# Attention over pooled keys and a gated feed-forward: three ways to raise a gate, two gate functions, and a new written-out order

## The chip, the cores and the metric

The kernel runs on one core of a Trainium2 chip. A core has five engines that each run their own instructions in order and meet through semaphores: TensorE (PE; its weight loads are shown apart as PEld), VectorE (DVE), ScalarE (ACT), GpSimd (POOL) and SyncE (SP), which issues transfers. ScalarE and GpSimd issue transfers on queues of their own as well. Matrix products land in PSUM, which has eight banks. The metric is the device time of one execution in microseconds, the median over runs; lower is better.

## The reference

Shapes: q, k and v are 8 batches x 8 heads x 576 rows x 64, w_in is 512 x 1024, conv_w is 3 x 1024, w_out is 1024 x 512, all float32; the output is 8 x 576 x 512 float32.

```
k_p = k.reshape(B, H, 72, 8, D).mean(axis=3)      # 576 rows -> 72
v_p = v.reshape(B, H, 72, 8, D).mean(axis=3)
scores = (q @ k_p.T) / sqrt(D)
attn = exp(scores - max(scores)); attn = attn / sum(attn)
x = concat_heads(attn @ v_p)                      # 576 x 512 per batch
h = relu(x @ w_in)                                # 576 x 1024
conv_out[s] = sum over k of conv_w[k] * h[s + k - 1]
out = (h * sigmoid(conv_out)) @ w_out
```

## The kernel before

The eight batches form four groups of two. A group's 1152 rows are nine tiles of 128 rows (group 0 is cut into ten, so that its first batch can start alone): 37 tiles of attention in all. For each tile the steps are, with the names and lines of the code before:

- `att_scores` (L530): the scores of all eight heads into two banks of PSUM, on PE.
- `att_max` (L571, instruction L575): the negated maximum of each head's 72 scores, on DVE.
- `att_shift` (L583): adds that maximum. On DVE (L587) it writes the shifted scores to `sd`; on PE (L595) two products with the identity add it in PSUM.
- `att_exp` (L605, instruction L613): one exponential over 128 x 576 on ACT, from `sd` or from PSUM.
- the turn of `e`: five transposes on PE (`att_turn`, L624) and a copy out of PSUM (`att_copy`, L638) by ACT or DVE, or one transposing transfer on SP's queue (`att_send`).
- `att_values` (L649) on PE, `att_divide` (L662, L664) on DVE.
- the turn of `x` in the same two ways: PE (L681) and a copy (L689), or a transfer (`att_out`).

Per batch the feed-forward follows, in eight blocks of 128 of the 1024 columns: `ffn_in` (L694, eight products per block), `ffn_relu` (L703, ACT), the convolution, the gate, and per group the output product `ffn_out` (L910), its copy (L921) and its store (L933, on SP or ACT). Blocks are gated four at a time; (b, f4) names the quarter-of-a-group gate of batch b, half f4.

The convolution of a gate is done in one of two ways. Either PE multiplies with 64 x 64 diagonal matrices (`ffn_conv`, L856), and then half of its results land on the other half of the partitions: ACT writes the tanh of the even blocks into `gT` and of the odd blocks into `tg` (L881), and the raise by one, on DVE, brings the halves of `tg` back to their place (L892, L894). Or it is done by taps: the first on ACT (L829), two on DVE (L831), tanh on ACT (L836), raise on DVE (L842). The second way is taken for (4,1), (5,0), (5,1), (6,0), (6,1) and (7,0). Either way the product with h follows on DVE (L902 or L843). The sigmoid is (1 + tanh(c/2))/2; the relu carries the factor one half. The convolution reads h past its ends from wrapped columns, which POOL copies for batches 4 to 7 (`ffn_wrap`, L778, L779).

The queries arrive as 64-column pieces that PE turns (L483, L487), and DVE or ACT copies them out (`qT`, L501). Keys are pooled with a product on PE (L373, L383) or in three halving sums on DVE (L406), values on DVE (L453), and masked copies of them are made (L457).

Nothing schedules itself: each step is entered into a graph, and the table ORDER names every step and its engine in the order of issue, FORMS the form of a product, PLACES the PSUM bank. An engine waits at its next row until the inputs have come and the buffer is free. Buffers are rings, and their counts stand in one line:

```
rings = {"e": 6, "eT": 3, "negm": 3, "x": 4, "tg": 3, "osb": 5, ...
```

## Time and profile before

| | |
|---|---|
| median of 3 runs | 219.06 us (218.57 to 219.35) |
| the profiled execution | 218.51 us, of which 216.8 us are its span |
| PE / DVE / ACT / POOL busy | 196.2 / 191.3 / 164.3 / 46.8 us |
| PE's granted clock, mean | 0.998 |
| moved by DMA | 32.62 MB, 150 GB/s |

The span is the time from the first to the last instruction of the program, and 1.7 us of the profiled execution lie around it. Busy time counts no register, semaphore or transfer-issuing instruction. A row of a group gives line, engine, operation, output <- input, shapes, count, then busy us and mean ns of one, then the idle time of the engine right before it and what released it. The chain that ended last is followed back from the last instruction, at each step to what released it.

### The profile page before, as it was taken

What the parts mean: (1) busy time and instruction counts of PE and PEld (TensorE: products, weight loads), DVE (VectorE), ACT (ScalarE), POOL (GpSimd) and SP (SyncE); (2) the same over time, 40 slices, a digit from 0 to 9 for tenths busy, and PEclk for the clock granted to TensorE, in tenths of its full rate; (3) what the DMA queues carried; (4) which work ended last, traced back from release to release, by engine and by line L of the source; (5) the groups of instructions that cost most, each with busy time, mean ns of one, the idle gap of its engine ahead of it and who ended that gap; (6) DMA issues with size and microseconds to landing.
All of it is one profiled execution on the core that took longest, in us unless ns stands there. A gap on an engine that the chain in (4) does not pass through costs nothing.

```text
span 216.8 us, 6589 instructions
## 1 busy us (share of the span) xinstructions
PE 196.2 (91%) x2718; PEld 136.2 (63%) x2736; DVE 191.3 (88%) x331; ACT 164.3 (76%) x277; POOL 46.8 (22%) x81
## 2 busy tenths in 40 slices
PE   0487999977999999979999999999999999999991
PEld 0455768866688886756676766676675656644540
DVE  7578987999999999998999999999999999999520
ACT  2057776899889889987578688889999989998220
POOL 7970335041103202000000013113305020530000
PEclk9999999999999999999999999999999999999999
DMA  5999999999999998997565665475576526315665
GB/s 78 156 186 202 208 205 208 207 208 206 206 207 206 205 210 128 178 129 168 115 94 115 137 72 131 83 153 102 115 154 136 134 59 155 81 36 135 150 178 183
DMA packets 48835, 32.62 MB, mean 150 GB/s; under 512 B 28301, under 2 KB 44325, under 8 KB 48805
## 3 DMA queue, kind: packets, MB, share of 16 engines
q0 software_dynamic: 16288, 16.26, 46.2%
q1 hardware_dynamic: 31636, 14.70, 33.5%
q10 hardware_dynamic: 880, 1.25, 2.1%
q8 instruction: 21, 0.34, 0.6%
q14 instruction: 10, 0.07, 0.1%
HBM read 32.52 MB, written 9.44 MB: 194 GB/s over the span
## 4 chain that ended last, share of the span: by engine, by line
PE 75%; DVE 9%; ACT 5%; issue 3%; POOL 3%; DMA 2%; DVEq 0%; POOLq 0%; ACTq 0%
PE psum L910 28%; PE psum L694 26%; PE psum L649 6%; PE psum L856 5%; DVE negm L575 3%; DMA eT<-e 2%; PE psum L624 2%; PE psum L549 2%; ACT qT L501 1%; DVE sd L587 1%; PE psum L681 1%; PE psum L562 1%; ACT eT L638 1%; PE psum L373 1%; PE psum L595 1%
## 5 line engine op out<-in xcount | busy, mean ns | idle before, releaser
L694 PE MATMUL psum<-xT,w_in_sb 128*128 128x288 bf16 x512 | 72.4, 286 | 0.1
L910 PE MATMUL psum<-w_out_sb,gT 128*128 128x512 bf16 (+1 forms) x278 | 66.2, 373 | 0.9 <-issue 0.2
L694 PEld LDWEIGHTS <-w_in_sb 128*128 128x128 bf16 x512 | 47.8, 98 | 15.6 <-issue 0.2
L703 ACT ACTIVATE hT<-psum 128x576 bf16<-128x576 f32 x64 | 40.5, 649 | 8.6 <-PE psum L694 7.0
L910 PEld LDWEIGHTS <-gT 128*128 128x128 bf16 x296 | 27.5, 98 | 26.1 <-issue 0.5
L831 DVE SCALAR_TENSOR_TENSOR tg<-hT,convw,tg 128x576 f32<-128x576 bf16 x48 | 37.2, 817 | 0.4
L575 DVE TENSOR_REDUCE negm<-psum 128x8 f32<-128x576 f32 (+2 forms) x37 | 27.2, 751 | 2.3 <-PE psum L562 1.0
L778 POOL COPY hT<-hT 128x126 bf16<-128x126 bf16 x16 | 9.3, 580 | 92.1 <-ACT hT L703 75.0
L664 DVE TENSOR_TENSOR x<-psum,r 128x512 bf16<-128x512 f32 (+1 forms) x37 | 25.6, 691 | 1.3
L587 DVE TENSOR_TENSOR sd<-psum,negm 128x576 f32<-128x576 f32 x27 | 20.0, 752 | 0.8
L649 PE MATMUL psum<-vm,eT 128*128 128x65 bf16 (+5 forms) x240 | 19.3, 222 | 1.4 <-DMA eT<-e 1.0
L856 PE MATMUL psum<-hT,dw 64*64 64x288 bf16 (+2 forms) x608 | 19.4, 261 | 0.5 <-DVE sd L587 0.3
L613 ACT ACTIVATE e<-sd 128x576 bf16<-128x576 f32 x27 | 18.4, 686 | 0.9 <-DVE sd L587 0.9
L856 PEld LDWEIGHTS <-dw 64*64 64x64 bf16 x608 | 15.4, 107 | 5.2 <-issue 4.3
L829 ACT ACTIVATE tg<-hT,convw 128x576 f32<-128x576 bf16 x24 | 18.4, 775 | 0.1
L649 PEld LDWEIGHTS <-eT 128*128 128x128 bf16 (+1 forms) x240 | 15.1, 100 | 5.3 <-DMA eT<-e 1.2
L921 ACT COPY osb<-psum 128x512 f32<-128x512 f32 x25 | 14.4, 586 | 4.9 <-PE psum L910 3.4
L836 ACT ACTIVATE gT<-tg 128x576 bf16<-128x576 f32 x24 | 16.2, 683 | 1.0 <-DVE tg L831 1.0
L881 ACT ACTIVATE gT<-psum 128x576 bf16<-128x576 f32 x20 | 13.0, 649 | 2.7 <-PE psum L856 2.5
L881 ACT ACTIVATE tg<-psum 128x576 bf16<-128x576 f32 x20 | 13.0, 651 | 2.2 <-PE psum L856 1.5
L902 DVE TENSOR_TENSOR gT<-gT,hT 128x2304 bf16<-128x2304 bf16 x10 | 13.6, 1359 | 0.0
L453 DVE TENSOR_TENSOR v<-v 128x1280 bf16<-128x1280 bf16 (+2 forms) x24 | 13.0, 541 | 0.3
(82 smaller groups left out, 228.6 us busy)
## 6 DMA issues: line engine op xcount, KB each, us to landing
out_dram<-osb SPq DMA_DIRECT2D x54, 128.0 KB, 2.4
v<-in_v_dram POOLq DMA_DIRECT2D x8, 512.0 KB, 19.3
qp<-in_q_dram POOLq DMA_DIRECT2D x7, 576.0 KB, 18.2
kk<-in_k_dram POOLq DMA_DIRECT2D x3, 1152.0 KB, 16.4
w_in_sb<-in_moe_w_in_dram POOLq DMA_DIRECT2D x2, 512.0 KB, 16.0
w_out_sb<-in_moe_w_out_dram POOLq DMA_DIRECT2D x1, 1024.0 KB, 22.0
out_dram<-qp SPq DMA_DIRECT2D x8, 128.0 KB, 2.6
out_dram<-qp ACTq DMA_DIRECT2D x8, 128.0 KB, 2.7
```

The lines of the kernel that those rows point to most:

```text
L575: nc.vector.tensor_reduce(out=a["m"][0:rows], in_=a["s"][0:rows, :, 0:2 * KW].rearrange("p a (h s) -> p a h s", s=Sp), axis=AX.X, op=OP.ma ...
L587: nc.vector.tensor_tensor(out=a["d"][0:rows], in0=a["s"][0:rows, :, 0:2 * KW].rearrange("p a (h s) -> p a h s", s=Sp), in1=a["m"][0:rows]. ...
L613: nc.scalar.activation(out=dst, in_=src, func=ACT.Exp, scale=1.0 / (POOL * 8.0),)
L649: nc.tensor.matmul(out=a["o"][lo:hi, h // 4, (h % 4) * (D + 1):(h % 4 + x1 - x0) * (D + 1)], lhsT=a["eT"][:, j, lo:hi], rhs=buf("vm", b)[: ...
L664: nc.vector.tensor_tensor(out=a["x"][0:rows].rearrange("p (a h d) -> p a h d", a=2, d=D), in0=ov[:, :, :, 0:D], in1=r[0:rows].unsqueeze(3) ...
L694: nc.tensor.matmul(out=banks(ps)[:, j, 0:SC], lhsT=w_in_block(dc, fb), rhs=buf("xT", g)[:, dc, i * S + j * SC:i * S + (j + 1) * SC], start ...
L703: nc.scalar.activation(out=h_of(b)[:, fb].rearrange("p (a s) -> p a s", a=2), in_=banks(ps)[:, :, 0:SC], func=ACT.Relu, scale=0.5,)
L829: nc.scalar.activation(out=acc, in_=h, func=ACT.Identity, scale=w)
L831: nc.vector.scalar_tensor_tensor(out=acc, in0=h, scalar=w, in1=acc, op0=OP.mult, op1=OP.add)
L856: nc.tensor.matmul(out=banks(pss[r ^ c])[c * D:(c + 1) * D, j, lo:hi], lhsT=dw[r * D:(r + 1) * D, tap * n_fb + fb, :], rhs=hT[r * D:(r + 1 ...
L881: nc.scalar.activation(out=t.rearrange("p (a s) -> p a s", a=2), in_=banks(ps)[:, :, 0:SC], func=ACT.Tanh, scale=0.5,)
L910: nc.tensor.matmul(out=bank(ps)[0:rows, columns], lhsT=buf("gT", g)[:, fb, t * P:t * P + rows], rhs=w_out_sb[:, fb, columns], start=(fb == 0),
```

## The change

1. *The raise of a gate* (`raise_gate`, new, L814). It may be done on ACT (L818, an Identity with a bias of one) as well as on DVE (L822). Its parts are no longer bound together: one row may stand apart from the next, with other work between. ACT does six raises in the program as built, five of 64 x 1152 and one of 128 x 1152.
2. *Swap by DMA* (`ffn_swap`, L900): two transfers put the halves of `tg` straight into `gT`, and one raise over all four blocks follows. The table "swap" names (3,0), (5,1), (6,0) and (6,1). The last three are gates by taps ("conv" is 1), and `add_taps` does not read "swap", so the program as built holds two such transfers, both for (3,0), issued on ACT.
3. *Sigmoid* instead of tanh for (5,0) to (7,1): no raise, relu without the half; an odd half of (7,1) is copied to its place (L820). All Sigmoids are ordered behind the last exponential, with one load of a second table of functions.
4. *The shift* ("shift"): by PE for 11 tiles (10 before), by eight exponentials of 72 columns each with the maximum as bias for three tiles, (1,6), (3,3) and (3,5), by DVE for 23 (27 before).
5. *The turns*: of `e` by transfer for 19 tiles (18 before), of `x` for 20 (18 before).
6. *Engines*: five of the 64 relus go from ACT to DVE. Between the two engines' copies out of PSUM, ACT has fewer (eT 15 full and 2 half to 12 and 1, xT 12 and 2 to 8 and 1, qT of 1152 columns 8 to 6, outputs 25 to 23 of `osb`), DVE more. Of the wraps POOL does 20 (32 before), ACT four, and (4,0) and (7,1) have none. ACT issues 24 transfers (11 before), SP ten stores fewer.
7. *Buffers*: e 6 to 4, tg 3 to 4, and the ring "s" goes. The pooling matrix lies in a buffer of `gT`. The factor of the scores moves from the exponential into the pooling matrix. Two products that only filled PE's time go.
8. *The order*: ORDER, FORMS and PLACES are written anew.

What the new order does, at three places. The first is DVE where the gates of batch 0 are raised and first multiplied (L902 before, L916 after); `kk` is the pooling of keys, `x` an attention result divided, `negm` a maximum, `sd` a shift. Before:

```order
L406 TENSOR_TENSOR kk_76<-kk_76 128x9x64
L892 TENSOR_SCALAR gT_119<-gT_119 128x2x576
L894 TENSOR_SCALAR gT_119<-tg_116 64x2x576 x2
L689 COPY xT_112<-psum 128x4x128
L902 TENSOR_TENSOR gT_119<-gT_119,hT_114 128x4x576
L575 TENSOR_REDUCE negm_93<-psum 128x8
```

After:

```order
L822 TENSOR_SCALAR gT_119<-tg_115 64x2x576
L697 RECIPROCAL r_109<-psum 64x8
L699 TENSOR_TENSOR x_104<-psum,r_109 64x512
L697 RECIPROCAL r_108<-psum 128x8
L699 TENSOR_TENSOR x_106<-psum,r_108 128x512
L598 TENSOR_REDUCE negm_96<-psum 128x8
L610 TENSOR_TENSOR sd_127<-psum,negm_96 128x576
L524 COPY qT_80<-psum 128x2x576
L598 TENSOR_REDUCE negm_96<-psum 128x8
L916 TENSOR_TENSOR gT_119<-gT_119,hT_113 128x4x576
```

Between the last raise and the product stand two divisions, two maxima, a shift and a copy of queries. Up to the first product DVE does four shifts and two maxima more than before.

The second is ACT at about the same time: the tanh of batch 0 (L881, L884) and the copies of batch 2's keys (`kT`) and queries (`qT`). Before:

```order
L881 ACTIVATE tg_117<-psum 128x576
L881 ACTIVATE gT_119<-psum 128x576
L689 COPY xT_112<-psum 128x4x64
L501 COPY qT_77<-psum 128x2x576
L501 COPY qT_79<-psum 128x2x576
L501 COPY qT_77<-psum 128x2x576
L501 COPY qT_79<-psum 128x2x576
```

After:

```order
L445 CAST kT_81<-psum 64x4x72 x2
L445 CAST kT_82<-psum 64x4x72 x2
L524 COPY qT_78<-psum 128x2x576
L524 COPY qT_80<-psum 128x2x576
L724 COPY xT_111<-psum 128x4x64
L724 COPY xT_111<-psum 128x4x128
L648 ACTIVATE e_98<-sd_127 128x576
L884 ACTIVATE tg_116<-psum 128x576
L884 ACTIVATE gT_119<-psum 128x576
```

Two copies of queries have left ACT here (DVE has them), and the last tanh of batch 0 stands behind the copies and an exponential.

The third is ACT at the last exponential (L613, L648) and the first gates behind it (L836 a tanh, L851 a Sigmoid). Before:

```order
L613 ACTIVATE e_97<-sd_126 128x2x2x144
L836 ACTIVATE gT_119<-tg_116 128x576
L613 ACTIVATE e_100<-sd_126 128x2x2x144
L921 COPY osb_125<-psum 128x512
L703 ACTIVATE hT_115<-psum 128x576 x2
```

After:

```order
L648 ACTIVATE e_97<-sd_126 128x2x2x144
L851 ACT_TABLE_LOAD
L851 ACTIVATE gT_119<-tg_116 128x576
L851 ACTIVATE gT_119<-tg_118 128x576
L745 ACTIVATE hT_113<-psum 128x576 x2
```

The table is loaded right behind the last exponential, and the gates by taps that stood among the exponentials stand behind it.

The diff, cut to its core:

```diff
-    rings = {"e": 6, "eT": 3, "negm": 3, "x": 4, "tg": 3, "osb": 5,
+    rings = {"e": 4, "eT": 3, "negm": 3, "x": 4, "tg": 4, "osb": 5,
...
+        "conv": {
+            (4, 1): 1, (5, 0): 1, (5, 1): 1, (6, 0): 1, (6, 1): 1, (7, 0): 1,
+        },
+        "swap": {
+            (3, 0): 1, (5, 1): 1, (6, 0): 1, (6, 1): 1,
+        },
...
+        "sigma": {
+            (5, 0): 1, (5, 1): 1, (6, 0): 1, (6, 1): 1, (7, 0): 1, (7, 1): 1,
+        },
...
     ORDER = (
-        6, 10, 2, 4, 28, 16, 14, 20, 24, 22, 34, 8, 26, 42, 36, 44, 12, 32, 30, 40, 92, 56, 18, 98, 38, 95, 58, 101, 104, 64,
+        6, 18, 28, 14, 16, 8, 2, 20, 10, 4, 34, 12, 108, 104, 36, 30, 22, 24, 40, 92, 32, 38, 97, 111, 56, 106, 98, 42, 95, 58,
...
     def att_exp(g, t):
         a, rows = att[g, t], rows_of(g, t)
         e = a["e"] = buf("e", g, t)
+        if graph.chosen("shift", g, t) == 2:
+            for x in range(2):
+                for h in range(4):
+                    at = h // 2 * 2 * KW + x * KW + h % 2 * Sp if a["by_rows"] else (4 * x + h) * Sp
+                    nc.scalar.activation(
+                        out=e[0:rows, at:at + Sp],
+                        in_=a["s"][0:rows, x, h * Sp:(h + 1) * Sp],
+                        func=ACT.Exp,
+                        bias=a["m"][0:rows, x, h:h + 1],
+                        scale=1.0,
+                    )
+            return
...
+    def gate_func(b, fb):
+        return ACT.Sigmoid if graph.chosen("sigma", b, fb // 4) else ACT.Tanh
+
+    def raise_gate(engine, b, fb, out, in_, start=0):
+        sigma = graph.chosen("sigma", b, fb // 4)
+        if engine is nc.scalar:
+            rows = slice(start, start + in_.shape[0])
+            nc.scalar.activation(out=out, in_=in_, func=ACT.Identity, bias=0.0 if sigma else ones[rows], scale=1.0)
+        elif sigma:
+            engine.tensor_copy(out=out, in_=in_)
+        else:
+            engine.tensor_scalar(out=out, in0=in_, scalar1=1.0, scalar2=None, op0=OP.add)
...
+    def ffn_swap(b, f4, queue):
+        g, i = where[b]
+        tg, gate = buf("tg", b, f4), buf("gT", g)[:, 4 * f4:4 * f4 + 4, i * S:(i + 1) * S]
+        gate = gate.rearrange("p (f e) s -> p e f s", e=2)[:, 1]
+        for part in range(2):
+            queue.dma_start(out=gate[part * D:(part + 1) * D], in_=tg[(1 - part) * D:(2 - part) * D])
...
+    for o in sigmas:
+        for e in exps:
+            graph.follow(e, o)
```

More of the change, by code (lines that the diff above doesn't have):

```diff
@@ L967, with add_load @@
[L967 to L980 removed]
+    n_outs = {b: [t for t in range(9) if (t < 4) == (i == 0)] for b, (g, i) in where.items()}
+    kb = H * S * D * 4
+    loads, kp, qp, qTt = {}, {}, {}, {}
+    kk0 = token("kk", 0)
+    kk = {0: kk0}
+    def add_load(kind, b, share=1.0, **part):
@@ L1014 @@
-    p0 = add({"POOL": 1.6}, first("pm"), build_pool_matrix, after=[c1])
-    add_load("q", 0, first("q0"), 4 / 9, cs=slice(0, 4))
-    c0 = add({"POOL": 0.55}, first("ident"), lambda: make_identity(nc, ident))
-    z0 = add({"DVE": 0.3}, soon(), lambda: clear(buffers["kT"][0]))
-    idf = add({"ACT": 0.3}, soon(), lambda: nc.scalar.copy(out=ident_f, in_=ident), after=[c0])
-    cwtok = token("ps")
-    cwp = add({"PE": 0.1}, soon(), lambda: turn_conv_weights(cwtok), after=[idf, cwl], uses=[cwtok], count=2)
@@ new lines, in add_out, with queue @@
+            then(o, lambda o, t=t, sm=sm: ffn_copy(g, t, sm, copier(o)))
+            o = add({"SP": 1.3, "ACT": 1.16}, None, after=[o], uses=[osb], land=(2.4, 0, 1))
+            then(o, lambda o, t=t: ffn_store(g, t, queue(o)))
+    def queue(o):
+        return nc.scalar if o.engine == "ACT" else nc.sync
+    for b in range(B):
+        if b < 2:
+            add_prep_k(b)
+        elif b % 2 == 0:
+            add_pair(b // 2)
+        add_prep_q(b)
+        add_prep_v(b)
+    for b in range(B):
+        for t in n_tiles[b]:
+            add_att(where[b][0], t)
@@ L1343 @@
+    for b in range(B):
+        add_ffn(b)
+        add_out(b)
+    for o in sigmas:
+        for e in exps:
+            graph.follow(e, o)
     with tc.manual_schedule():
```

832 lines of the change are left out of this document (387 added, 445 removed), and 100 rows, old and new, of tables (ORDER, PLACES).

## The prediction

> **What bounds the kernel now.** I read the page's first lines, then busy time by stage, then the chain that ended last, then the groups by shape. The page first:
>
> ```profile
> span 216.8 us, 6589 instructions
> PE 196.2 (91%) x2718; PEld 136.2 (63%) x2736; DVE 191.3 (88%) x331; ACT 164.3 (76%) x277; POOL 46.8 (22%) x81
> PE 75%; DVE 9%; ACT 5%; issue 3%; POOL 3%; DMA 2%; DVEq 0%; POOLq 0%; ACTq 0%
> ```
>
> TensorE carries three quarters of the chain, but VectorE is almost as full, so the share alone decides nothing. The view by stretches, cut where the work changes (PE, PEld, DVE, ACT and POOL busy, each with its count, the granted clock, the DMA share and GB/s):
>
> ```profile
> 0.00:40.00 40.00, 29.06 (x578) 22.61 (x579) 31.12 (x77) 22.47 (x39) 20.55 (x38) 1.00 1.12 179
> 40.00:60.00 20.00, 17.60 (x331) 13.36 (x334) 19.31 (x32) 18.26 (x31) 3.87 (x5) 1.00 1.23 207
> 60.00:92.00 32.00, 31.81 (x562) 25.20 (x560) 30.95 (x57) 29.41 (x50) 4.41 (x6) 1.00 1.13 189
> 92.00:152.00 60.00, 58.35 (x852) 40.78 (x862) 57.79 (x98) 46.64 (x80) 6.63 (x14) 1.00 0.64 118
> 152.00:203.00 51.00, 50.43 (x358) 29.57 (x365) 49.62 (x67) 45.42 (x77) 11.32 (x19) 1.00 0.52 116
> 203.00:217.00 14.00, 8.96 (x49) 4.66 (x48) 2.50 (x4) 2.13 (x4) 0.00 (x0) 0.97 0.58 162
> ```
>
> From 60 to 203 us TensorE idles 0.19 + 1.65 + 0.57 = 2.4 us. A gain must therefore come from less work for it, or from the 10.9 us that it idles before 40, the 2.4 between 40 and 60, and the 1.65 after 92. The chain names what ends those waits (start, duration, engine, tile, line):
>
> ```profile
> 16.40 0.42 PE psum L595 x2
> ...
> 49.48 3.15 ACT qT L501 x3
> ...
> 61.80 0.39 PE psum L624 x5
> 62.18 0.98 PE psum L694 x8
> ...
> 73.61 0.41 PE psum L681 x4
> ...
> 90.59 0.46 DVE gT L894
> ...
> 92.04 4.25 DMA eT<-e
> ...
> 196.72 9.88 PE psum L910 x49
> 206.66 5.37 PE psum L910 x28
> 212.05 0.42 DVE qp L921
> ```
>
> Around 50 ScalarE's copies of the queries stand in the chain, ahead of 92 VectorE's gates, at 92 one turned tile on its way by DMA. The end is TensorE's output product, one copy, and stores.
>
> **The change, part by part.** VectorE first, by shapes (busy us, mean ns, then idle before):
>
> ```profile
> L587 DVE TENSOR_TENSOR sd<-psum,negm 128x576 f32<-128x576 f32 x27 | 20.0, 752 | 0.8
> L894 DVE TENSOR_SCALAR gT<-tg 64x1152 bf16<-64x1152 bf16 x20 | 9.1, 455 | 0.3
> L842 DVE TENSOR_SCALAR gT<-gT 128x2304 bf16<-128x2304 bf16 x6 | 4.7, 790 | 0.4 <-ACT gT L836 0.3
> L892 DVE TENSOR_SCALAR gT<-gT 128x1152 bf16<-128x1152 bf16 x10 | 4.5, 451 | 0.0
> L689 DVE COPY xT<-psum 128x512 bf16<-128x512 bf16 x5 | 2.1, 418 | 0.0
> L501 DVE COPY qT<-psum 128x1152 bf16<-128x1152 bf16 x2 | 1.5, 752 | 0.0
> L921 DVE COPY osb<-psum 128x512 f32<-128x512 f32 x2 | 1.4, 680 | 0.0
> L638 DVE COPY eT<-psum 128x640 bf16<-128x640 bf16 x2 | 1.0, 480 | 0.0
> ```
>
> It loses four shifts (27 to 23), 4 x 0.752 = 3.0. The raises of the gate by one are 9.1 + 4.7 + 4.5 = 18.3 now; afterwards 13 of the half shape, 7 of 1152 and 2 of 2304 columns remain, 5.9 + 3.2 + 1.6 = 10.7, so 7.6 less. It gains five relus out of PSUM, an operation it has no row for: between the 0.680 of a smaller PSUM copy and the 0.817 of a multiply-add, I take the shift's 0.752, the same shape out of PSUM, 3.8 in all. Copies taken from ScalarE: 2.5 of eT 1.2, 2.5 of xT 1.0, two of qT less a short one 1.1, two of outputs 1.4, half an output and a key some 0.9. Sum: -10.6 + 9.4 = -1.2 us.
>
> ScalarE's rows:
>
> ```profile
> L703 ACT ACTIVATE hT<-psum 128x576 bf16<-128x576 f32 x64 | 40.5, 649 | 8.6 <-PE psum L694 7.0 <-DVE x L664 0.8
> L613 ACT ACTIVATE e<-sd 128x576 bf16<-128x576 f32 x27 | 18.4, 686 | 0.9 <-DVE sd L587 0.9
> L921 ACT COPY osb<-psum 128x512 f32<-128x512 f32 x25 | 14.4, 586 | 4.9 <-PE psum L910 3.4 <-remote 1.0 <-PE psum L649 0.3
> L638 ACT COPY eT<-psum 128x640 bf16<-128x640 bf16 x15 | 10.1, 695 | 1.3 <-PE psum L624 1.3
> L501 ACT COPY qT<-psum 128x1152 bf16<-128x1152 bf16 x8 | 8.6, 1125 | 0.8 <-PE psum L483 0.8
> L689 ACT COPY xT<-psum 128x512 bf16<-128x512 bf16 x12 | 7.0, 592 | 0.4 <-PE psum L681 0.2
> L1018 ACT ACT_TABLE_LOAD x1 | 1.3, 1283 | 0.8 <-PEq L1359 0.8
> L398 ACT CAST kT<-psum 64x144 bf16<-64x144 f32 x4 | 1.0, 273 | 6.8 <-DVE kT L294 6.2 <-PE psum L373 0.6
> 204.01 2.50 ACTq L933 DMA_DIRECT2D out_dram<-qp  x4
> ```
>
> It loses five relus (3.2), three whole exponentials net (2.1), 3.5 copies of eT (2.4), 4.5 of xT (2.6), two of qT less one short (1.7) and some 3 other copies (1.9): 13.9. It gains 24 short exponentials, for which the nearest row is the smallest evacuation, 273 ns: 6.6 (lower end 0.2 each, if they overlap as the relus do, 4.8); one table load 1.3; eight short wrap copies by the same 273 ns, 2.2; six raises by the qT row, the nearest of that width, 6 x 1.125 = 6.8; and 13 more transfers issued on its queue at 2.50 / 4 = 0.63 each, 8.1, which are not counted as busy but hold the engine. Sum: +25.0 - 13.9 = +11 us. That leaves ScalarE at 164.3 + 6.9 for the eleven issues of today + 11 = 182 of 217, still not the fullest. The cover is its idle time of 13.4 us between 92 and 152, and 5.6 after it; without that cover each of those operations delays TensorE.
>
> The sixfold raise on ScalarE is dearer in every row: on VectorE the same six are 5 x 0.455 + 0.451 = 2.7. The Trainium skill, "ScalarE: Activation LUTs", section "Rules for kernel authors", says to use VectorE, not ScalarE, for add and multiply. By that rule this part costs 4 us of engine time for nothing; the sum stands at zero for it, because VectorE is the fuller engine here, and by the rule, with ScalarE on the path, it would be up to 4 us worse. No row of before has a raise on ScalarE.
>
> The load of the second table stands between the last exponential and the first Sigmoid. Priced by its row it is 1.3 us once. The same page, section "What ACT_TABLE_LOAD costs", adds a drain of about 1.38 us to the 1283 ns; the row agrees with the 1283, and no row here shows the drain. With it the switch would be an estimated 2.7 us, and ScalarE's sum +12.4.
>
> TensorE, by the chain's rows: one turn of e less (0.39), two of x less (0.82), one shift more (0.42): -0.8. The two fillers that go stand in its idle start and are worth nothing. The turns become transfers, one more of eT and two more of xT, each on SP, whose queue loses ten stores; how a late one hurts the row at 92 shows (4.25 us).
>
> The swap by DMA reaches one gate only: the table names four, but the other three are tap gates, whose code never reads it. For gate (3,0) two transfers on ScalarE's queue replace two half raises and a whole one (1.36) by one raise (0.79) after landing. Their price as latency is bounded by nothing and 4.25, the slowest transfer in the chain; VectorE's taps and maxima and TensorE's input products of the next batch cover it, so zero. POOL gives up 12 wraps and was 78% idle: zero. Fewer buffers for e (6 to 4): an exponential waits for the turn four tiles before it instead of six; the row L613 shows 0.9 us of waits now, all for VectorE's shifts, so zero, with another 0.9 as upper end. The start, from the timeline of POOL:
>
> ```profile
> 5.13 1.33 POOL L319 TENSOR_SCALAR_AFFINE_SELECT mask<-mask 128x15 bf16<-128x15 bf16 x2
> 6.42 1.64 POOL L298 TENSOR_SCALAR_AFFINE_SELECT gT<-gT 64x648 bf16<-64x648 bf16 x2
> ```
>
> POOL now builds the pooling matrix (L298) ahead of the mask. TensorE's first pooling can start 1.3 earlier, VectorE's use of the mask comes 1.6 later; VectorE has as much work before the first maximum as now, so I take zero between -1.3 and +1.6.
>
> Two places remain that the order decides. At 40 to 60 ScalarE has two qT copies less (-2.1 us of the chain's row at 49.48), while VectorE has more ahead of its first gate product: four shifts and two maxima of 0.75 (4.5), copies (0.9) less a few clears (0.4), so 5.0 us. TensorE has, ahead of its first output product, two turns (0.8), an input product (0.98) and more score products, some 2.1 in all. The place is worth between -2.4 (TensorE's idle time gone) and 5.0 - 2.1 = +2.9. The middle is +0.2; I take 0, since VectorE idled between 12 and 40 and can take part of its extra there. At 92 between 0 and -1.65; I take half, -0.8, because other tiles now stand there.
>
> Sum: -0.8 - 0.8 = -1.6. The profiled execution lasted 218.51 (216.8 of span and 1.7 around it), 216.9 by this sum; it lies 0.55 below the median of 219.06, so the median comes to **217.4**. Its own range is 215.4 to 218.4.
>
> **Rivals.** *The order closes the stalls.* The idle 2.4 at 40 to 60 and all 1.65 at 92 go, with TensorE's 0.8: 219.06 - 4.85 = 214.2, and 211.4 if 2.8 of the idle time before 40 goes too. For it: ScalarE's chain at 49.48 is shorter. Against it: VectorE's 19.31 of 20 there.
>
> *VectorE's gates come late in the first stage* (the other side). The 5.0 us more ahead of the first product L902 find no idle time, TensorE arrives 2.1 later and waits 2.9: 219.06 - 0.8 + 2.9 = 221.2. It decides once VectorE absorbs less than 2.1 of the 5.0 in its waits before 40 us. For it: 97% of that stage. Against it: VectorE is lighter afterwards, yet TensorE, dense from 60 on, could not regain what it lost.
>
> *ScalarE becomes the bound.* The Sigmoids wait for the last exponential, ScalarE has 5.6 us free from 152 to 203, and 1.3 of load, one or two raises and four issues (1.3 + 2.2 + 2.5 = 6.0) fill it. If 2.5 reach TensorE: 219.06 - 0.8 + 2.5 = 220.8.
>
> *The parts cancel*: within 0.3% (0.66 us) of 219.06, the bound of what a measurement of this kernel tells from no change.
>
> **How the numbers follow.** 0.44 for the forecast, 0.17 for closed stalls, 0.22 for late gates, 0.11 for ScalarE, 0.06 for cancelling. Faster: 0.44 + 0.17 less 0.02 at the forecast's edge = 0.59; slower: 0.22 + 0.11 less 0.02 that end near zero = 0.31; the same 0.10. The range takes the forecast, most of the stalls' case and both slower ones with their bounds: 211.8 to 221.9.
>
> **What would show it.** TensorE near 195.4 busy, VectorE near 190, ScalarE near 167; the raises on ScalarE near 1.1 us and short exponentials between 0.2 and 0.27; a second table load of 1.28 with ScalarE idle before it or not; two transfers tg to gT and no more; TensorE idle under 2 us between 60 and 203. I am wrong if TensorE idles over 4 us between 40 and 60 waiting for VectorE (late gates), if ScalarE is named as the releaser of TensorE after 150, or if the first maximum comes later than 13 us.

## The result and the profile after

The changed kernel took **225.6 us** (median of 5 runs, 224.97 to 225.68) beside 219.06 us (218.57 to 219.60) for the kernel before: a ratio of 1.0295, 95% interval 1.0262 to 1.0327. It is 6.5 us slower where 1.6 us of gain were forecast, and above the range. The profiled execution lasted 225.55 us, 223.8 of them span. A run's time goes with the mean clock that it is granted: in two sets of runs the changed kernel took 224.9 to 225.7 us in the seven at 0.994 or more (median 225.55), and 227.4 to 228.0 in the four at 0.988 to 0.991.

The page's first lines after:

```profile
span 223.8 us, 6596 instructions
PE 199.2 (89%) x2712; PEld 137.9 (62%) x2729; DVE 190.7 (85%) x327; ACT 164.3 (73%) x290; POOL 36.8 (16%) x70
PE 62%; DVE 14%; ACT 7%; DMA 7%; issue 5%; SPq 2%; POOL 1%; ACTq 0%; DVEq 0%; POOLq 0%
```

VectorE and ScalarE are close to what was forecast. No engine became the bound. What changed is the chain: TensorE's share fell from 75% to 62%; transfers, the issue of transfers on SP and plain "issue" took 14% of it against 5% before, and VectorE 14% against 9%. So the loss is waiting. The view by stretches, cut as before, says where (PE, PEld, DVE, ACT and POOL busy, granted clock, DMA share, GB/s):

```profile
0.00:40.00 40.00, 29.70 (x518) 23.36 (x519) 32.16 (x77) 22.37 (x37) 19.84 (x39) 1.00 1.11 179
40.00:60.00 20.00, 18.43 (x373) 14.09 (x374) 19.60 (x34) 18.49 (x35) 3.11 (x4) 1.00 1.23 207
60.00:92.00 32.00, 28.89 (x511) 22.13 (x515) 28.60 (x54) 24.50 (x43) 5.11 (x7) 1.00 1.04 167
92.00:152.00 60.00, 55.29 (x843) 38.45 (x843) 53.54 (x88) 44.52 (x84) 1.18 (x4) 1.00 0.77 132
152.00:203.00 51.00, 50.68 (x401) 32.09 (x406) 46.16 (x63) 46.92 (x82) 7.54 (x16) 1.00 0.48 105
203.00:224.00 21.00, 16.21 (x82) 7.75 (x81) 10.60 (x15) 7.53 (x13) 0.00 (x0) 0.97 0.63 163
```

Between 60 and 92 TensorE idles 3.11 us (0.19 before), between 92 and 152 it idles 4.71 (1.65 before). VectorE lost its density in the same two places: 28.6 of 32 and 53.5 of 60. The DMA share rose from 0.64 to 0.77 in the second one. TensorE's waits, the costliest first:

```profile
PE psum L506 <- DMA qp<-in_q_dram: 5.7, 1, 5.7
PE psum L394 <- DMA kk<-in_k_dram: 2.2, 2, 1.8
PE psum L510 <- issue: 1.8, 1, 1.8
PE psum L572 <- DMA qT<-qp: 1.5, 1, 1.5
PE psum L729 <- ACT hT L745: 1.2, 1, 1.2
```

The first two lie in the idle start, which the kernel before has too. The other three are new; none stood in the forecast. Each has its place in the timeline. The 1.8 us lie inside one run of 64 x 64 products that turn queries of batch 5:

```profile
78.93 0.47 PE L510 MATMUL psum<-ident,qp 64*64 64x64 bf16 x34
81.21 0.22 PE L510 MATMUL psum<-ident,qp 64*64 64x64 bf16 x2 [1.81 <-issue]
...
107.31 0.32 PE L572 MATMUL psum<-kT,qT 64*64 64x72 bf16 x16 [1.51 <-DMA qT<-qp]
...
111.20 3.23 ACTq L905 DMA_DIRECT2D gT<-tg  x2
...
114.48 0.65 ACT L745 ACTIVATE hT<-psum 128x576 bf16<-128x576 f32 x1 [3.37 <-DMA gT<-tg]
...
115.18 1.63 PE L729 MATMUL psum<-xT,w_in_sb 128*128 128x288 bf16 x12 [1.23 <-ACT hT L745]
```

The second is a score product that waits for queries turned by transfer (L518). The third is the swap (L905): from the start of its first transfer's issue to the end of its second's, ScalarE is held for 3.2 us (the two issues take 0.68 and 0.63, and 1.93 lie between them), the next relu waits 3.37 us, and TensorE waits 1.23 us for that relu. SP's queue at that time shows what the turned queries waited for:

```profile
95.27 2.64 SPq L668 DMA_TRANSPOSE eT<-e  x2
98.01 3.74 SPq L708 DMA_TRANSPOSE xT<-x  x2
101.92 2.70 SPq L518 DMA_TRANSPOSE qT<-qp  x1
104.72 1.23 SPq L708 DMA_TRANSPOSE xT<-x  x1
106.12 1.48 SPq L668 DMA_TRANSPOSE eT<-e  x1
107.69 3.39 SPq L518 DMA_TRANSPOSE qT<-qp  x1
111.17 1.18 SPq L947 DMA_DIRECT2D out_dram<-osb  x2
```

SP is hardly free in these 17 us. One turn by transfer holds the queue for 1.2 to 2.1 us, one of queries 2.7 to 3.4. A full queue is not new: between 90 and 113 us SP issues for 20.8 of the 23 us, and in the kernel before for 20.3. What is new is the place of the queries, behind the turns. In the kernel before, the first turn of queries stood at 83 us, ahead of four stores, the second at 95.9, and no wait of TensorE names either (timeline of SP, before):

```profile
83.05 5.40 SPq L495 DMA_TRANSPOSE qT<-qp  x1
88.50 3.49 SPq L933 DMA_DIRECT2D out_dram<-osb  x4
```

How late the program is at a batch can be put in one number: the moment at which the relu of one block of that half begins, less the durations of all TensorE's work that the order puts up to that block's input product. It rises wherever TensorE lost time. The durations are one value for each kind of product, so a difference between two columns is an estimate, good to some half a microsecond. The feed-forward of batch 3 runs ahead of that of batch 2 in every kernel here. The last two columns belong to experiments below.

| relu of | before | after | four edits | five edits |
|---|---|---|---|---|
| batch 0, first half | 14.4 | 16.5 | 16.1 | 15.5 |
| batch 1, first half | 17.5 | 19.3 | 19.0 | 18.3 |
| batch 1, second half | 18.1 | 23.0 | 20.8 | 20.1 |
| batch 3, second half | 18.8 | 24.0 | 22.6 | 21.2 |
| batch 2, first half | 21.5 | 28.1 | 23.4 | 22.0 |
| batch 4, second half | 22.2 | 29.2 | 25.6 | 23.8 |
| batch 5, second half | 23.5 | 31.7 | 27.0 | 25.2 |
| batch 7, second half | 23.3 | 31.9 | 27.1 | 25.3 |

After against before, 2.1 us are lost by the first batch, 3.1 more between 65 and 83 us (both halves of batch 1), 1.7 more up to batch 2; at batch 5 the loss is 8.2 and at the end 8.6. Less the 1.1 us of TensorE's work that the change saves, that is 7.5, against 7.0 of span. The stretch of the late gates by Sigmoid, behind batch 5, loses 0.4.

### The profile page after: what moved, and what is told of

The parts are those of the page before. It is cut to its first block, busy times and chain, and to the rows that moved or that the text cites. A ratio compares the mean times of both kernels' runs of the same rounds, so it can differ in the third digit from the quotient of the medians.

```text
span 223.8 us, 6596 instructions
## 1 busy us (share of the span) xinstructions
PE 199.2 (89%) x2712; PEld 137.9 (62%) x2729; DVE 190.7 (85%) x327; ACT 164.3 (73%) x290; POOL 36.8 (16%) x70
## 4 chain that ended last, share of the span: by engine, by line
PE 62%; DVE 14%; ACT 7%; DMA 7%; issue 5%; SPq 2%; POOL 1%; ACTq 0%; DVEq 0%; POOLq 0%
PE psum L924 24%; PE psum L729 23%; PE psum L869 5%; DVE negm L598 3%; PE psum L684 3%; DMA kk<-in_k_dram 3%; DMA eT<-e 2%; DVE x L699 2%; DVE kk L426 2%; ACT hT L745 2%; SPq L518 2%; PE psum L572 1%; DVE sd L610 1%; PE psum L585 1%; DMA out_dram<-osb 1%
## 5 line engine op out<-in xcount | busy, mean ns | idle before, releaser
L924 PE MATMUL psum<-w_out_sb,gT 128*128 128x512 bf16 (+1 forms) x279 | 65.2, 373 | 1.3 <-issue 0.3
L745 ACT ACTIVATE hT<-psum 128x576 bf16<-128x576 f32 x59 | 37.7, 652 | 11.5 <-PE psum L729 7.6
L924 PEld LDWEIGHTS <-gT 128*128 128x128 bf16 x296 | 28.0, 98 | 28.2 <-DVE gT L916 0.6
L598 DVE TENSOR_REDUCE negm<-psum 128x8 f32<-128x576 f32 (+3 forms) x37 | 27.5, 751 | 7.3 <-PE psum L572 4.5
L699 DVE TENSOR_TENSOR x<-psum,r 128x512 bf16<-128x512 f32 (+1 forms) x37 | 25.6, 691 | 1.5 <-DVE r L697 0.2
L792 POOL COPY hT<-hT 128x126 bf16<-128x126 bf16 x10 | 4.8, 477 | 112.8 <-ACT hT L745 112.8
L916 DVE TENSOR_TENSOR gT<-gT,hT 128x2304 bf16<-128x2304 bf16 x16 | 21.5, 1353 | 0.7 <-ACT gT L851 0.4
L869 PE MATMUL psum<-hT,dw 64*64 64x288 bf16 (+2 forms) x640 | 18.8, 256 | 0.5 <-ACT tg L884 0.2
L869 PEld LDWEIGHTS <-dw 64*64 64x64 bf16 x640 | 15.5, 107 | 4.8 <-issue 2.6
L610 DVE TENSOR_TENSOR sd<-psum,negm 128x576 f32<-128x576 f32 (+1 forms) x23 | 17.3, 754 | 0.9
L851 ACT ACTIVATE gT<-tg 128x576 bf16<-128x576 f32 x24 | 16.0, 681 | 2.7 <-DVE tg L846 2.4
L648 ACT ACTIVATE e<-sd 128x576 bf16<-128x576 f32 (+1 forms) x23 | 15.9, 696 | 1.2 <-DMA eT<-e 0.7
L884 ACT ACTIVATE gT<-psum 128x576 bf16<-128x576 f32 x20 | 13.0, 655 | 3.1 <-PE psum L869 3.1
L884 ACT ACTIVATE tg<-psum 128x576 bf16<-128x576 f32 x20 | 13.1, 656 | 2.8 <-PE psum L869 2.6
L935 ACT COPY osb<-psum 128x512 f32<-128x512 f32 x23 | 13.2, 593 | 0.6 <-PE psum L924 0.6
## 6 DMA issues: line engine op xcount, KB each, us to landing
kk<-in_k_dram POOLq DMA_DIRECT2D x3, 1152.0 KB, 17.8
```

What stands on the lines that cost most here:

```text
L598: nc.vector.tensor_reduce(out=a["m"][0:rows], in_=a["s"][0:rows, :, 0:2 * KW].rearrange("p a (h s) -> p a h s", s=Sp), axis=AX.X, op=OP.ma ...
L610: nc.vector.tensor_tensor(out=a["d"][0:rows], in0=a["s"][0:rows, :, 0:2 * KW].rearrange("p a (h s) -> p a h s", s=Sp), in1=a["m"][0:rows]. ...
L699: nc.vector.tensor_tensor(out=a["x"][0:rows].rearrange("p (a h d) -> p a h d", a=2, d=D), in0=ov[:, :, :, 0:D], in1=r[0:rows].unsqueeze(3) ...
L745: nc.scalar.activation(out=out, in_=banks(ps)[:, :, 0:SC], func=ACT.Relu, scale=scale)
L869: nc.tensor.matmul(out=banks(pss[r ^ c])[c * D:(c + 1) * D, j, lo:hi], lhsT=dw[r * D:(r + 1) * D, tap * n_fb + fb, :], rhs=hT[r * D:(r + 1 ...
L884: nc.scalar.activation(out=t.rearrange("p (a s) -> p a s", a=2), in_=banks(ps)[:, :, 0:SC], func=gate_func(b, fb), scale=0.5,)
```

## The experiments

Each experiment has its ratio to the kernel before, measured with it on the same chip, and beside it the median of its runs at a mean granted clock of 0.993 or more, with their count. The last column says by how much that median lies below the 225.55 of the changed kernel. The kernel before, at that clock, took 219.8 us in the set of the first four experiments and 218.6 to 219.1 in the other three sets; the second value of the last column allows for this (225.55 is scaled to the set's time of the kernel before). The two values differ by up to 0.8 us, so a single effect is known no better than that; where a single run is left, nothing under 1 us is read from it.

| run | ratio to before (95%) | us at clock 0.993 or more | below the changed kernel, us |
|---|---|---|---|
| changed kernel, measured again (e9_after) | 1.0382 (1.0332 to 1.0431) | 225.55 (7, both sets) | - |
| queries of batch 5 in half form | 1.0242 (1.0169 to 1.0315) | 224.06 (3) | 1.5, 2.3 |
| no swap | 1.0264 (1.0196 to 1.0333) | 224.84 (3) | 0.7, 1.5 |
| turned queries sent earlier | 1.0360 (1.0291 to 1.0429) | 226.41 (1) | -0.9, -0.1 |
| these three together | 1.0182 (1.0127 to 1.0238) | 223.32 (3) | 2.2, 3.0 |
| six buffers of e | 1.0276 (1.0229 to 1.0323) | 224.40 (4) | 1.1, 0.8 |
| one exponential for eight | 1.0327 (1.0289 to 1.0364) | 224.96 (1) | 0.6, 0.2 |
| tanh for the Sigmoids | 1.0422 (1.0373 to 1.0471) | 226.06 (1) | -0.5, -0.9 |
| raises on VectorE | 1.0329 (1.0263 to 1.0395) | 225.23 (3) | 0.3, 0.0 |
| three turns back on TensorE | 1.0258 (1.0205 to 1.0310) | 224.44 (5) | 1.1, 0.6 |
| four edits | 1.0159 (1.0134 to 1.0185) | 222.16 (6) | 3.4, 2.9 |
| three shifts back on TensorE | 1.0326 (1.0275 to 1.0378) | 225.04 (3) | 0.5, 0.5 |
| five edits | 1.0113 (1.0075 to 1.0152) | 221.71 (6) | 3.8, 3.8 |
| five edits, raises and exponentials undone | 1.0247 (1.0211 to 1.0283) | 224.79 (6) | 0.8, 0.8 |

### The queries of batch 5 in the half form

The two query turns of batch 5 take 18 products of 128 columns each instead of 36 of 64:

```diff
-L510 MATMUL psum<-ident,qp_75 64x64      (36 for each of the two)
+L506 MATMUL psum<-ident,qp_75 64x128     (18 for each of the two)
```

> The changed kernel with one thing undone: the queries of batch 5 are turned by 36 products of half width (HALF) instead of 72 small ones, twice. In the changed kernel TensorE stands still for 2.0 us at 79.2 in the middle of the 72, with no semaphore named. Theory A (its instructions come too slowly: the wait lies between two products of one run, and a 16 KB transfer on the queue for instructions starts at 78.85): the wait goes, 225.6 falls to about 224 (-2.0 and +0.4 for the wider form). Rival B (the data or a buffer are late there): the wait stays in another place, 225.6 to 226.

The timeline of TensorE at the place of the stall, in this run:

```profile
78.77 0.70 PE L506 MATMUL psum<-ident,qp 128*64 128x128 bf16 x18
79.40 0.32 PE L572 MATMUL psum<-kT,qT 64*64 64x72 bf16 x16
```

The turn takes 0.70 us where it took 2.5, from 78.93 to 81.43, and no wait is left in it. (The expectation counts twice as many products; 36 and 18 are those of the trace.) TensorE is busy 31.01 of the 32 us between 60 and 92, against 28.89; this profile had a granted clock of 0.95 throughout, but the run with three edits below, at full clock, has 30.91. The time fell by 1.5 us (224.06 against 225.55), or 2.3 by the second value: its theory A, 224.

What TensorE waited for, the profile calls "issue" only. The transfers on the queue for instructions, which theory A named, point to it. In all ten profiles that keep the small form the stall ends 2.2 to 2.4 us after a 16 KB transfer on that queue begins (78.85 and 81.21 us in the changed kernel), whether it lasted 0.9 or 2.4 us, and in nine of the ten it stands behind the 34th of the 36 products. The 36 small products at 75.44 us run through in 0.51 us. So the instructions of this place came late, as far as timing can show it; small products alone do not stall. The edit changes form and count of instructions together and doesn't separate the two.

### The one gate without the swap

Gate (3,0) gets the three raises of its kind instead of two transfers and one raise.

```diff
-ups.append(then(o, lambda o: ffn_swap(b, f4, queue(o))))
-ups += add_raise(b, f4, raised(1, 2304), lambda o: ffn_raise(b, slice(4 * f4, 4 * f4 + 4), hand(o)), ...
+ups.append(then(o, lambda o: None))
+ups += add_raise(b, f4, raised(1, 2304), lambda o: [ffn_gate(b, f4, part, hand(o)) for part in (2, 0, 1)], ...
```

> The changed kernel without the swap by DMA: gate (3,0) is raised by three instructions on VectorE in the place where the one raise stood, in the same order. Theory A (the second transfer of the swap holds ScalarE's queue from 111.2 to 114.4, because it waits for an earlier transfer to land, and TensorE waits 1.2 us for the relu behind it): ScalarE's wait of 3.4 us goes, TensorE's 1.4 with it, 225.6 falls to 223.8 to 224.4. Rival B (ScalarE would wait there anyway, for TensorE): 225.3 to 225.8.

ScalarE's wait of 3.37 us for the transfer and TensorE's for the relu behind it are gone, and TensorE is busy more between 92 and 116 us (first after, then this run):

```profile
92.00:116.00 24.00, 20.57 (x324) 14.82 (x321) 20.54 (x34) 14.19 (x24) 0.00 (x0) 1.00 0.95 170
```

```profile
92.00:116.00 24.00, 22.74 (x362) 16.07 (x348) 21.30 (x37) 16.95 (x28) 0.00 (x0) 1.00 0.93 169
```

Of these 2.2 us 0.7 to 1.5 reach the time (224.84). The swap costs, though it is one gate of sixteen. The chain of the changed kernel tells how it could hold ScalarE for so long:

```profile
107.69 3.39 SPq L518
...
111.17 2.62 DMA out_dram<-osb
...
113.81 0.63 ACTq L905
...
115.16 1.25 ACT gT L818
```

The swap's second transfer, on ScalarE's queue, was released by a store that SP had issued at 111.17, behind the transfer of queries. The two have no data in common. In the trace every transfer from SP or ScalarE has one of the same eight semaphores, and the swap's second transfer waits for the one whose last user was that store, which landed at 113.79 us. So a store on SP can hold ScalarE.

### The turned queries sent earlier

The transfer that turns the queries of batch 6 for the score product at 107 us is moved up by five places on SP.

```diff
+L518 DMA_TRANSPOSE qT_78<-qp_73 128x18x128
 L708 DMA_TRANSPOSE xT_112<-x_104 128x4x128
 L668 DMA_TRANSPOSE eT_101<-e_99 128x5x128
...
 L708 DMA_TRANSPOSE xT_112<-x_106 128x4x128
-L518 DMA_TRANSPOSE qT_78<-qp_73 128x18x128
```

> The changed kernel with one row moved: the transposing transfer of the queries of batch 6 stands on SP's queue 5 transfers earlier (ahead of the first turn of x of group 1 by transfer). Theory A (TensorE's 1.5 us wait at 107 for these queries is SP's order): the wait goes, 225.6 falls to about 224. Rival B (the queue is full there, and what moves back by 2.7 us is missed instead): 225.3 to 227.

The waits of TensorE and ScalarE in this run:

```profile
PE psum L924 <- ACT osb L935: 1.5, 1, 1.5
```

```profile
ACT e L635 <- DMA eT<-e: 4.8, 1, 4.8
ACT osb L935 <- DMA out_dram<-osb: 2.1, 1, 2.1
```

The wait for queries at 107 us is gone, and a wait of the same 1.5 us stands at 101 us instead: an output product waits for ScalarE's copy, and that for an earlier store. Nothing was gained: another place on the same full queue moved the wait, as its rival B had it.

### The three together

> The changed kernel with all three edits of this set: half-width turning of the queries of batch 5, no swap by DMA, the queries of batch 6 sent earlier. If the three waits are separate and all are on TensorE's path, their gains add: 225.6 - 1.6 - 1.4 - 1.5 = 221.1. If one wait only hides the next, less than half of it: 223.5 or more. Before is 219.06.

223.32 us, 2.2 less than the changed kernel and the sum of the first two (1.5 and 0.7). The third gave nothing here either, and the 221.1 of added gains was not reached.

### Six buffers of e

```diff
-    rings = {"e": 4, "eT": 3, ...  "qp": 4, ...
+    rings = {"e": 6, "eT": 3, ...  "qp": 3, ...
```

> The changed kernel with six buffers for e in place of four (the slots handed out anew, the oldest free one each time; room comes from one of four query buffers that nothing uses). Same order. Theory A (ScalarE's 3.8 us wait at 141 for a transfer that still reads the buffer, and a good part of TensorE's loss from 120 to 160, come from four buffers): the wait goes, 225.6 falls by 1.5 to 2.5. Rival B (those exponentials are early enough, TensorE loses there for other reasons): within 0.5 of 225.6.

The wait of an exponential for a turn by transfer (3.80 us at 144.88 in the changed kernel) is gone. The time is 224.40, 0.8 to 1.1 less, with single runs from 223.8 to 225.9: near the upper end of 0.9 that the prediction gave, between its theory and its rival, and not separable from a smaller value.

### One exponential, one table, raises on VectorE

Three runs undo ScalarE's added work, one piece each. In the first, the three tiles get one exponential without the maximum; in the second, all gates take tanh and no second table is loaded, but the six late gates are left without their raise; in the third, the six raises go to VectorE.

```diff
-        if graph.chosen("shift", g, t) == 2:
+        if False:
```

```diff
-        return ACT.Sigmoid if graph.chosen("sigma", b, fb // 4) else ACT.Tanh
+        return ACT.Tanh
```

```diff
-L818 ACTIVATE gT_119<-tg_116,ones 64x2x576        (ACT, six in all)
+L822 TENSOR_SCALAR gT_119<-tg_116 64x2x576        (DVE)
```

> The changed kernel with one exponential straight from PSUM, without the maximum, in place of the eight short ones for tiles (1,6), (3,3) and (3,5); it leaves out subtracting the maximum for these three tiles. Each takes some 1.2 us less of ScalarE (1.80 to about 0.6). Theory A (ScalarE's length there is not what TensorE waits for): 225.3 to 225.8. Rival B (ScalarE is what bounds from 110 to 150): 225.6 falls by 1 to 2.5.

> The changed kernel with Tanh for Sigmoid in the six late gates, so that no second table is loaded; it leaves the six gates at tanh without the raise, and the order, which holds them behind the last exponential, is the same. Theory A (TensorE is dense behind 152 and the switch of 1.3 us, or 2.7 if the page on the tables is right about a drain, is hidden): within 0.4 of 225.6. Rival B (the Sigmoids bound the end): 1.3 to 2.7 us faster.

> The changed kernel with the six raises of ScalarE done by VectorE, each in its old place in the order (1.25 us on ScalarE against 0.45 on VectorE by the rows of after). Theory A (ScalarE in order: what stands behind a raise waits, as the relu at 116): 0.5 to 1.2 us faster. Rival B (VectorE is the fuller engine and passes the delay on): 0 to 0.8 us slower.

None of the three gained what can be measured: 224.96 (one run), 226.06 (one run) and 225.23 against 225.55. In the second, the stretch from the end of the last exponential to the end is as long as in the changed kernel (58.8 and 58.7 us); its profiled run lost time ahead of any edited instruction, where the granted clock was one half from 82.0 to 85.4 us. ScalarE's rows in the changed kernel (by shape, then its timeline) have about the costs that the prediction gave them, and no gain shows from undoing them here:

```profile
L635 ACT ACTIVATE e<-psum,negm 128x72 bf16<-128x72 f32 x24 | 5.4, 338 | 3.8 <-DMA eT<-e 3.8
L818 ACT ACTIVATE gT<-tg,ones 64x1152 bf16<-64x1152 bf16 x4 | 5.0, 1252 | 0.1
```

```profile
144.88 1.80 ACT L635 ACTIVATE e<-psum,negm 128x72 bf16<-128x72 f32 x8 [3.80 <-DMA eT<-e]
...
164.44 0.68 ACT L648 ACTIVATE e<-sd 128x576 bf16<-128x576 f32 x1
165.13 1.28 ACT L851 ACT_TABLE_LOAD   x1
166.43 0.68 ACT L851 ACTIVATE gT<-tg 128x576 bf16<-128x576 f32 x1
```

Eight exponentials take 1.80 us in a row, and the load stands between the last exponential and the first Sigmoid with no gap on either side.

### Three turns back on TensorE

Of the changed turns, e of tile (1,1) and x of (1,0) and (1,2) are turned on TensorE as before, with copies on ScalarE and VectorE.

```diff
-L708 DMA_TRANSPOSE xT_112<-x_104 128x4x128
 L668 DMA_TRANSPOSE eT_101<-e_99 128x5x128
-L668 DMA_TRANSPOSE eT_103<-e_100 128x5x128
 L708 DMA_TRANSPOSE xT_111<-x_105 128x4x128
-L708 DMA_TRANSPOSE xT_112<-x_106 128x4x128
 L518 DMA_TRANSPOSE qT_78<-qp_73 128x18x128
```

> The changed kernel itself, as the measure for the two others of this set: 1.0295 times before, within 0.5%.

> The changed kernel with three of the four added turns by transfer done on TensorE: e of tile (1,1), x of (1,0) and (1,2), with their copies on ScalarE (one) and VectorE (two). TensorE has 1.2 us more to do. Theory A (the three transfers stand in SP's queue between 93 and 102, ahead of the queries of batch 6, which TensorE waits for at 107, and set back what comes behind): the queries go out some 4 us earlier, the waits at 107 go, and the time falls by 1 to 2.5 against the changed kernel. Rival B (SP catches up): 0 to 1.2 slower.

The changed kernel measured again came to a ratio of 1.0382, outside the 0.5% of its expectation; at the clock of the table its two runs, 224.92 and 224.93, are 1.029 times the 218.56 of the kernel before.

In the run with the three turns on TensorE the queries go out at 98.55 us instead of 101.92. TensorE's wait for them (1.5) is gone, and its wait for the relu behind the swap is 0.4 instead of 1.2, although neither the queries' transfer nor the swap was touched:

```profile
PE psum L510 <- issue: 1.5, 1, 1.5
PE psum L585 <- ACT tg L884: 0.8, 2, 0.4
PE psum L572 <- ACT qT L524: 0.6, 1, 0.6
```

```profile
92.00:116.00 24.00, 22.61 (x360) 15.97 (x354) 21.50 (x36) 16.38 (x28) 0.00 (x0) 1.00 0.92 167
```

At equal clock the time fell by 0.6 to 1.1 us (224.44), while TensorE does 1.2 us more work. The turns ahead of the queries on SP are shown as the cause of the wait for queries. For the swap they are not: its issue still holds ScalarE for 3.02 us, from 109.83, but the relu behind it now waits for its own input product, which ends at 112.82, so the hold no longer reaches TensorE.

### Four edits

Half form, no swap, turns on TensorE and six buffers of e.

> The changed kernel with four things undone: the queries of batch 5 turned at half width, no swap by DMA, the three turns of group 1 on TensorE, six buffers for e. If these are the separate causes (2.0, 1.4, 1.5 and 0.5), 5.4 us less than the changed kernel, about 1.005 times before; if the rest of the loss is in the order itself, 2.5 to 4 less, 1.011 to 1.018 times before.

222.16 us, 3.4 less than the changed kernel; the single effects, 1.5, 0.7, 1.1 and 1.1, add up to 4.4, so they overlap (2.9 of 5.2 by the second values). The ratio of 1.0159 is in the range of the expectation's second reading, that the rest of the loss lies in the order itself. Another 3.3 against the 218.8 of before were left.

### The start, and all together

Three early tiles, (0,5), (0,6) and (0,9), get their shift from TensorE again, alone and on top of the four edits. The last run gives the raises to VectorE and takes one exponential for eight on top of that, to see whether the other waits had only covered ScalarE's work.

```diff
-            (0, 0): 1, ... (0, 4): 1, (0, 7): 1, (0, 8): 1, ...
+            (0, 0): 1, ... (0, 4): 1, (0, 5): 1, (0, 6): 1, (0, 9): 1, (0, 7): 1, (0, 8): 1, ...
```

> The changed kernel with one edit: the shift by the row maximum of the three tiles (0,5), (0,6) and (0,9) is added by TensorE, as in the kernel before, and not by VectorE (0.45 us each, some 1.4 us in all, which stand ahead of the first feed-forward products; those begin 2.4 us later than before). Theory A (VectorE's added work makes the start late, and with it all that follows): the relus of the first feed-forward batch come 1 to 2 us earlier than in the changed kernel (32.2 us to 30 or 31), and the time falls by 1 to 2 us, to 223.5 to 224.5 against 225.0 to 225.6 in runs of equal clock. Rival B (the start is set by loads and by the written order, or its delay is swallowed by the waits behind it): less than 0.5 us.

> The four edits of the earlier run together (queries of batch 5 turned in the half form, no swap in the one gate that has it, the three added turns by DMA back on TensorE, six buffers of e), which took 222.2 us, and the edit of the start besides. Theory A: what stays open of the loss, some 3.4 us, begins at the start (1.8 us there), so the time comes to 220 to 221. Rival B (the start's delay isn't VectorE's): 222 or more.

> The five edits, and the two that gave nothing by themselves: one exponential instead of eight for each of the three tiles (without the maximum's subtraction for them) and the six raises of gates on ScalarE given to VectorE. Theory A (the added work of ScalarE was covered by the other waits only, and shows once they are gone): 1 us or more below the run with five edits. Rival B (it is hidden still, at a last product that waits for TensorE): within 0.5 us of it, or above.

The first feed-forward product comes at 30.1 us with the shifts on TensorE, 31.0 in the changed kernel and 28.6 before. But this moment varies with the loads: in the profiles with an unedited start it lies between 29.8 and 31.1. Counted from the first maximum it comes 16.1 us later in the kernel before, 17.7 to 18.4 in all with the unedited start, and 17.8 and 18.1 with the shifts on TensorE. The time fell by 0.5 us in both comparisons (225.04 against 225.55, 221.71 against 222.16), no more than single runs differ (224.9 to 226.6 in the first). So the start is late by some 2 us, and that VectorE's shifts are a piece of it is not shown. (A shift on VectorE takes 0.75 us by its row, L610, not the 0.45 of the expectation.)

With five edits TensorE waits for hardly anything after its start:

```profile
PE psum L506 <- POOL gT L316: 5.8, 1, 5.8
PE psum L394 <- DMA kk<-in_k_dram: 1.2, 2, 0.9
PE psum L716 <- DVE x L699: 0.6, 2, 0.4
PE psum L869 <- DVE sd L610: 0.6, 1, 0.6
```

The last run is above the five edits, as its rival B allowed, but by 3.1 us (224.79 against 221.71, six runs each), which neither theory had reckoned with. The engines' busy time, first with five edits, then in the last run, and three of TensorE's waits there:

```profile
PE 201.4 (92%) x2712; PEld 138.5 (63%) x2712; DVE 190.0 (86%) x330; ACT 165.5 (75%) x291; POOL 37.0 (17%) x70
```

```profile
PE 201.3 (90%) x2712; PEld 138.4 (62%) x2712; DVE 192.8 (86%) x336; ACT 155.5 (70%) x264; POOL 36.8 (17%) x70
```

```profile
PE psum L869 <- DVE sd L610: 1.1, 1, 1.1
PE psum L659 <- DVE qT L524: 0.7, 1, 0.7
PE psum L684 <- DVE sd L610: 0.7, 1, 0.7
```

ScalarE is 10.0 us lighter, VectorE 2.8 heavier, and the kernel 3.1 slower. All of TensorE's waits of 0.3 us or more that name VectorE add up to 5.3 us in the last run and to 2.4 with five edits, which is nearly the whole difference. So with the other waits gone TensorE waits for VectorE, and the raises on ScalarE, 1.25 us each against 0.455, look like a gain there. The run carries two edits, and only the raises add to VectorE; that they are the cause was not measured by itself.

What stays open is 2.6 us between the five edits and the kernel before (221.71 against 219.07). By the table above 1.1 us are lost at the start and 0.9 more by the second half of batch 1; TensorE also has 0.9 us more work than in the kernel before, by the durations of its rows. What makes the start late wasn't found. No version was found that beats the kernel before.

## Why the prediction was wrong

- **"The turns become transfers ... each on SP, whose queue loses ten stores."** This is the step that failed: a term of the sum with the wrong sign. Where the added turns stand, between 90 and 113 us, SP was full before (20.3 of 23 us) and after (20.8); the three hold it for 1.2 to 1.6 us each, and the queries of batch 6 behind them come late. The prediction counted TensorE's saving of 0.39 + 0.82 and nothing for the queue. Undoing the three turns gained 0.6 to 1.1 us: the step cost that much and did not gain 1.2.
- **The swap: "so zero".** The count was right, two transfers and one gate. The price was taken as the latency of the gate, covered by VectorE's other work. The cost lay on the issuing engine: ScalarE was held for 3.2 us, 1.9 of them for a store on SP, with a relu behind it. Measured 0.7 to 1.5 us. The prediction's own upper end, 4.25, was wide enough; the choice of zero looked at who waits for the gate and not at what stands behind the issue.
- **A cost that the sum left out.** The forms of the two query turns of batch 5 (in the kernel before one of them was small already) were part of "FORMS ... written anew", and no term priced them. They cost 1.5 to 2.3 us, the largest single piece, by a stall that ends with a transfer of instructions and that no row of before shows; its largest wait of this kind was 0.4.
- **Fewer buffers of e: "zero, with another 0.9 as upper end".** 0.8 to 1.1 measured, loosely; the upper end was the better value, for the exponential waits for a turn by transfer, and those were late. The row of waits quoted for it (0.9, all for VectorE) came from a kernel in which no exponential waited for a turn.
- **"The start ... zero between -1.3 and +1.6".** The first maximum came at 12.85 us, 0.3 later than before and under the limit of 13, so the reordering on POOL is as forecast. But the first feed-forward product came 2.4 us later (31.0 against 28.6), and batch 0 is 2.1 late in the table. "VectorE has as much work before the first maximum as now" looked at the first maximum only; what counts is the work ahead of the first feed-forward product. What of it makes the start late stays open; taking three shifts off VectorE gave 0.5 us at most.
- **"At 40 to 60 ... I take 0".** This held. The first gate product came 2.9 us later and the first output product 3.5, but the delay was brought along from the start: the table has +2.1 at batch 0 and +1.8 at batch 1. TensorE idled 1.57 us there, less than the 2.40 before, not the over 4 that would have spoken for the rival of late gates.
- **"TensorE idle under 2 us between 60 and 203".** Failed: 3.1 + 4.7 + 0.3 = 8.1. This is the line that shows the loss most plainly.
- **The place at 92: "half, -0.8".** The wait of before went, but three others took its place between 78 and 116.
- **ScalarE's costs.** The raises took 1.25 us (1.125 forecast), eight short exponentials 1.80 (2.2 forecast), the table load 1.28 with no idle time before it. They seem hidden, as the forecast had it: undoing them one at a time gained nothing clear, though for two of them a single run is left to tell by. The rule of the Trainium skill that the prediction weighed, VectorE and not ScalarE for additions ("ScalarE: Activation LUTs", "Rules for kernel authors"), agrees with the two engines' durations, 0.455 and 1.25. It did not decide the time: with the raises on VectorE and one exponential for eight, the kernel with five edits was slower by 3.1. The drain that the Trainium skill adds to a table load (the same page, "What ACT_TABLE_LOAD costs") shows nowhere here: the load starts right behind the last exponential, and the first Sigmoid 0.02 us behind the load.
- **The rival of ScalarE as the bound** had the wrong place. ScalarE did hold TensorE, most of all at 115 us (1.2) through the swap, not after 152 through the Sigmoids, where TensorE idled 0.3 us in all.
- **Busy time.** TensorE was busy 199.2, not 195.4, though its work is less; the busy time of pipelined products holds waits too and was no good mark.

The forecast treated each transfer as a latency with somebody else's work to cover it, and left out what stands behind it on the queue that issues it; the rivals held engines only, none a queue. Undoing five pieces brought back 3.8 of the 6.5 us, two of them, the turns and the swap, such transfers. The 2.6 that remain lie in the new order, and which part of it costs them stays open.

## What to carry to other kernels

When work moves from an engine to transfers, add up what the issuing queue then holds in the stretch where it is used (here 1.2 to 3.4 us for a turn), what then comes late behind it, and not only the latency of one transfer. Look at what stands behind the issue on that engine, and at which earlier transfer it must wait for. An engine that is slower at a task can still be its right place, when the others wait for the faster one. And undo a part again after the waits around it are gone: here the raises, undone alone, changed nothing that could be measured, and undone with the exponentials on top of five edits the kernel lost 3.1 us.

## What the runs showed of the chip

- TensorE can stall inside one run of products without any wait that the profile names: for 1.8 us among 36 products of 64 x 64 in the changed kernel, for 0.9 to 2.4 in the nine other profiles with that form, and not at all with half as many products of twice the width. The stall ended 2.2 to 2.4 us after a 16 KB transfer on the queue for instructions began, in all ten. Why that transfer began too late just here is not settled; other transfers of the kind passed without a stall.
- Two engines' queues are tied to each other through the semaphores that their transfers share: an issue on ScalarE was held for 1.9 us by a store on SP with other data (0.7 to 1.5 us of this kernel's time, with the rest of the swap).
- The granted clock can drop behind such a stall. In the three profiles in which it lasted 2.1 to 2.4 us, the clock is one half for 3.4 us, beginning 80.5 to 82.0 us into the span, about where the stall ends; in the seven with 0.9 to 1.8 us it is not. Of all runs of the programs with that form 27 of 55 had a mean clock under 0.993, of those with the half form 2 of 26. What the drop costs was not measured by itself.
